# A cross network's input loads rearranged: the second half's remainder transposed on VectorE, fewer transfers on SyncE

## The chip, the cores and the metric

The kernel runs on one core of a Trainium2 chip. The metric is the device time of one execution in microseconds (us). TensorE does the matrix products, ScalarE moves sums out of PSUM and adds a bias, VectorE does the elementwise products and sums, GpSimd makes a few small copies, SyncE issues most of the transfers (DMAs). ScalarE has a queue of its own on which it issues transfers, in order with its other instructions.

## The reference

```python
B, D, L = 4096, 416, 6              # x0: B x D, ws: L x D x D, bs: L x D, all bfloat16
x = x0
for l in range(L):
    x = x0 * (x @ ws[l] + bs[l]) + x
```

## The kernel before, in words

Layers 0 to 4 work on x transposed: features lie on the partitions and rows of the batch along the free axis. The 416 features are three blocks of 128 (the *main* part, XM, index m for an output block and k for an input block) and a *remainder* of 32 (XR). The 4096 rows are two halves s = 0, 1 of four groups g of 512 rows. As 32 features fill only a quarter of the partitions, XR stacks the four groups: partition 32g + r holds feature r of group g. XRd is a copy of XR with its upper and lower 64 partitions exchanged, which the first layer uses for m = 1. The last layer turns round and makes rows of the output directly, from X0rows (x0 as it lies in memory), XLrows (the transposed x of the last layer) and bLr (the last bias row, on partitions 0, 32, 64 and 96).

The loads. SyncE issues, in this order: transposing loads of x0's main part into XM[0] (L75, eight of 512 rows), with the second half's remainder as rows (xrem, L84) after the fifth; weights of layer 1 (L71), the weights' remainder rows (L90), weights of layers 2 to 5, one load for each; x0's rows in four loads (L123); the last bias row in four (L125). ScalarE's queue issues the weights of layer 0, the biases, the first half's remainder in four loads (xrig, L80) and the remainder row of layer 0's weights (WR, L87), which L108 and L110 then copy to three more groups of partitions.

The remainder gets its transposed form in `x0_rem`: four TensorE transposes of a 128x128 tile into PSUM (L155), then one VectorE copy to XR[0] and two to XRd (L158). For the first half the tiles come straight from the four loads; for the second half, GpSimd first copies xrem into their order (L132).

The first layer, `first_layer(s)`, runs for each half. Its PSUM tiles come from a pool of four buffers of 1024 columns (`psum`). pa[0] to pa[2] are the sums of output blocks 0 to 2 for groups 0 and 1, pb[0] to pb[2] those for groups 2 and 3, pr the remainder's. `full` multiplies main blocks (L212), `row` adds the remainder's share (L219). ScalarE empties a tile (`ew_main`, L163), VectorE multiplies by x0 (L164) and adds x (L167); `ew_rem` does the same for pr (L171 to L173). The first half's `x0_rem` stands between the first and second group's products, the second half's behind the first half's pr (`mm_rem`, L191 and L196). Layers 1 to 4 follow in tiles of the same kind (L179, L185), and the last layer (L325 to L353).

The program's scheduler may move instructions of an engine against each other as long as their data allow. `tc.keep_in_program_order(ins)` ties an instruction behind the one that was written before it on its engine; it adds no wait between engines. Each transfer signals its end on one of eight completion semaphores, which are given out in turn in the order of the schedule.

Of the kernel before, what the change touches and what calls it, by code (L numbers as in the profile page):

```python
# [11 lines left out]
BF16 = mybir.dt.bfloat16  # L12
# [4 lines left out]
def kernel(  # L17
# [7 lines left out]
    nc = tc.nc  # L25
    B, D = x0.shape
    L = ws.shape[0]
    P = 128
    NK = 3
    R = D - NK * P  # L30
    assert R == 32 and B == 4096 and D == 416 and L >= 2
    NS = 2
    NG = 4
    CW = 512
    SW = NG * CW
    NBT = B // P
    LL = L - 1

    const = ctx.enter_context(tc.tile_pool(name="const", bufs=1))
    big = ctx.enter_context(tc.tile_pool(name="big", bufs=1))  # L40
# [4 lines left out]
    x0_v = x0.rearrange("(bt p) d -> p bt d", p=P)  # L45
    out_v = out.rearrange("(bt p) d -> p bt d", p=P)

    ident = const.tile([P, P], BF16)
    dz = const.tile([P, 2], FP32)
    ones = const.tile([P, P], BF16)  # L50
    WM = const.tile([P, L, NK, D], BF16)
# [3 lines left out]
    bLr = const.tile([P, D], BF16)  # L55
    bM = const.tile([P, NK, L], FP32)
    bR = const.tile([P, L], FP32)
    X0rows = big.tile([P, NBT, D], BF16)
    XLrows = big.tile([P, NBT, D], BF16)
    scrR = [big.tile([P, 4, P], BF16, name=f"scrR{s}") for s in range(NS)]  # L60
    xrem = big.tile([P, 16, R], BF16)
    xrig = big.tile([P, NS, 4, P], BF16)
    XRd = big.tile([P, NS * CW], BF16)
    XM = [big.tile([P, NK, B], BF16, name=f"XM{i}") for i in range(3)]
    XR = [big.tile([P, NS * CW], BF16, name=f"XR{i}") for i in range(3)]

    def col0(s, g):
        return SW * s + CW * g

    def load_wm(eng, l):  # L70
        eng.dma_start(WM[:, l], ws[l, 0:NK * P, :].rearrange("(k p) n -> p k n", p=P))  # L71

    def load_x0t(s, g):
        c0 = col0(s, g)
        nc.sync.dma_start_transpose(out=XM[0][:, :, c0:c0 + CW], in_=x0[c0:c0 + CW, 0:NK * P])  # L75

    def load_xrem0():
        with nc.allow_non_contiguous_dma(reason="64B row segments"):
            for i in range(4):
                nc.scalar.dma_start(xrig[:, 0, i, :].rearrange("p (g r) -> p g r", g=NG), x0_v[:, i:16:4, NK * P:D])  # L80

    def load_xrem1():
        with nc.allow_non_contiguous_dma(reason="64B row segments"):
            nc.sync.dma_start(xrem[:], x0_v[:, 16:32, NK * P:D])  # L84

    def load_wr0():
        nc.scalar.dma_start(WR[0:R, 0, :], ws[0, NK * P:D, :])  # L87
# [1 line left out]
    def load_wr(eng, g, l0, l1):  # L89
        eng.dma_start(WR[32 * g:32 * g + 32, l0:l1, :], ws[l0:l1, NK * P:D, :].rearrange("l r n -> r l n"))  # L90
# [9 lines left out]
    nc.scalar.dma_start(bsb[:], bs[:, :])  # L100
    load_x0t(0, 1)
    load_xrem0()
    load_wr0()
    nc.scalar.activation(dz[:, 1:2], dz[:, 0:1], ACT.Identity, bias=dz[:, 0:1], scale=1.0)  # L104
    for g in range(1, NG):
        dst, src = WR[32 * g:32 * g + 32, 0, :], WR[0:R, 0, :]
# [4 lines left out]
    for g in range(2, NG):  # L111
        load_x0t(0, g)
    load_x0t(1, 0)
    load_xrem1()
    for g in range(1, NG):
        load_x0t(1, g)
    load_wm(nc.sync, 1)
    for g in range(NG):
        load_wr(nc.sync, g, 1, L)
    for l in range(2, L):  # L120
        load_wm(nc.sync, l)
    for q in range(4):
        nc.sync.dma_start(X0rows[:, 8 * q:8 * q + 8, :], x0_v[:, 8 * q:8 * q + 8, :])  # L123
    for g in range(NG):
        nc.sync.dma_start(bLr[32 * g:32 * g + 1, :], bs[LL:LL + 1, :])  # L125

    def fill_wd(l0, l1):
        for g in range(NG):
            nc.gpsimd.tensor_copy(WD[32 * g:32 * g + 32, l0:l1, g, :], WR[32 * g:32 * g + 32, l0:l1, NK * P:D])

    fill_wd(0, 1)
    nc.gpsimd.tensor_copy(xrig[:, 1].rearrange("p i (g r) -> p i g r", g=NG), xrem[:].rearrange("p (g i) r -> p i g r", g=NG))  # L132
    fill_wd(1, L)

    wps = psum.tile([P, CW], FP32, tag="ps", name="wps")
# [14 lines left out]
        nc.vector.tensor_copy(bM[:], pb[:, 0:NK, 0:L])  # L150
        nc.vector.tensor_copy(bR[:], pb[:, 3, 0:L])

    def x0_rem(s, tpr):
        for i in range(4):
            nc.tensor.transpose(tpr[:, 128 * i:128 * i + 128], xrig[:, s, i, :], ident[:])  # L155
        for dst, src in ((slice(0, P), slice(0, P)), (slice(64, P), slice(0, 64)), (slice(0, 64), slice(64, P))):
            to = XR[0] if dst == src else XRd
            nc.vector.tensor_copy(to[dst, CW * s:CW * s + CW], tpr[src])  # L158

    def ew_main(l, s, m, h, pt, cur, nxt, pin=False):  # L160
        c0 = col0(s, 2 * h)
        t = tpool.tile([P, 2 * CW], BF16, name="t")
        nc.scalar.activation(t[:], pt[:].rearrange("p a b -> p (a b)"), ACT.Identity, bias=bM[:, m, l:l + 1], scale=1.0)  # L163
        prod = nc.vector.tensor_tensor(out=t[:], in0=t[:], in1=XM[0][:, m, c0:c0 + 2 * CW], op=ALU.mult)  # L164
        if pin:
            tc.keep_in_program_order(prod)
        nc.vector.tensor_tensor(out=nxt[:, m, c0:c0 + 2 * CW], in0=t[:], in1=cur[:, m, c0:c0 + 2 * CW], op=ALU.add)  # L167

    def ew_rem(l, s, pr, curR, nxtR):
        tr = tpool.tile([P, 2 * CW], BF16, name="t")  # L170
        nc.scalar.activation(tr[:, 0:CW], pr, ACT.Identity, bias=bR[:, l:l + 1], scale=1.0)  # L171
        nc.vector.tensor_tensor(out=tr[:, 0:CW], in0=tr[:, 0:CW], in1=XR[0][:, CW * s:CW * s + CW], op=ALU.mult)  # L172
        nc.vector.tensor_tensor(out=nxtR[:, CW * s:CW * s + CW], in0=tr[:, 0:CW], in1=curR[:, CW * s:CW * s + CW], op=ALU.add)  # L173
# [15 lines left out]
    def mm_rem(l, s, pr, cur, curR):  # L189
        for g in range(NG):  # L190
            nc.tensor.matmul(pr[32 * g:32 * g + 32, :], lhsT=WD[:, l, g, :], rhs=curR[:, CW * s:CW * s + CW],  # L191
                             start=True, stop=False, tile_position=(0, 32 * g))
        for k in range(NK):
            for g in range(NG):
                c0 = col0(s, g)
                nc.tensor.matmul(pr[32 * g:32 * g + 32, :], lhsT=WM[:, l, k, NK * P:D], rhs=cur[:, k, c0:c0 + CW],  # L196
                      start=False, stop=(k == NK - 1), tile_position=(0, 32 * g))
# [8 lines left out]
    def first_layer(s):  # L206
        cur, curR, nxt, nxtR = XM[0], XR[0], XM[1], XR[1]

        def full(pt, m, h, gl, after_row):
            c0 = col0(s, 2 * h + gl)  # L210
            for k in range(NK):
                nc.tensor.matmul(pt[:, gl, :], lhsT=WM[:, 0, k, 128 * m:128 * m + 128], rhs=cur[:, k, c0:c0 + CW],  # L212
                                 start=(k == 0 and not after_row), stop=(k == NK - 1 and after_row))

        def row(pt, m, h, opens):
            for gl in range(2):
                rg = 32 * ((2 * h + gl) ^ (2 if m == 1 else 0))
                src = XRd if m == 1 else curR
                nc.tensor.matmul(pt[:, gl, :], lhsT=WR[rg:rg + 32, 0, 128 * m:128 * m + 128],  # L219
                                 rhs=src[rg:rg + 32, CW * s:CW * s + CW],  # L220
                                 start=opens, stop=not opens, tile_position=(rg, 0))

        def ph(m):
            return psum.tile([P, 2, CW], FP32, tag="ps", name=f"ph{m}")

        pa = [ph(m) for m in range(NK)]
        if s == 0:
            for m in range(NK):
                full(pa[m], m, 0, 0, False)
            tp0 = psum.tile([P, CW], BF16, tag="ps", name="tpr")  # L230
            x0_rem(0, tp0[:])
            for m in range(NK):
                full(pa[m], m, 0, 1, False)
        else:
            for m in range(NK):
                for gl in range(2):
                    full(pa[m], m, 0, gl, False)
        pb = [ph(0)]
        row(pa[0], 0, 0, False)
        row(pb[0], 0, 1, True)  # L240
        row(pa[2], 2, 0, False)
        row(pa[1], 1, 0, False)
        for m in range(NK):
            ew_main(0, s, m, 0, pa[m], cur, nxt)
        for m in range(NK):
            if m:
                pb.append(ph(m))
            for gl in range(2):
                full(pb[m], m, 1, gl, m == 0)
        row(pb[1], 1, 1, False)  # L250
        row(pb[2], 2, 1, False)
        pr = psum.tile([P, 2, CW], FP32, tag="ps", name="pr")
        mm_rem(0, s, pr[:, 0, :], cur, curR)
        if s == 0:
            x0_rem(1, pr[:, 1, :].bitcast(BF16)[:, 0:CW])
        for m in range(NK):
            ew_main(0, s, m, 1, pb[m], cur, nxt, pin=(s == 0))
        ew_rem(0, s, pr[:, 0, :], curR, nxtR)
# [3 lines left out]
    for s in range(NS):  # L262
        first_layer(s)
# [49 lines left out]
    l = LL  # L313
# [97 lines left out]
```

## Time and profile before

| what | value |
|---|---|
| median of 3 runs | 130.69 us (130.51 to 130.90) |
| profiled execution | 130.58 us |
| its span, first to last instruction | 128.8 us |
| granted TensorE clock | 1.000 over the span |
| first layer, both halves | about 5.8 to 26.8 us |
| layers 1 to 4 | 26.8 to 103.7 us |
| last layer and stores | 103.7 to 128.8 us |
| DMA engines' busy share, 3 to 38 us | 0.9 or more in each slice |
| xrem's load | issued at 10.31 us, landed 4.6 us later |

A row of a timeline gives the start, the duration, the engine, the line, the operation, the tile written and the tile read; a "q" behind an engine's name marks its sequencer, which issues transfers and handles semaphores, and [..] is the engine's idle time before the row and what ended it. "x4" is the number of instructions that the row merges. In the chain of waits each row is a piece of the work that ended last.

### The profile page before, as it was taken

The numbers are of one execution on the slowest core, as the hardware profiler recorded it, in microseconds if no ns is written. First come the engines' busy times: TensorE is split into PE (matmuls) and PEld (weight loads), VectorE is DVE, ScalarE is ACT, GpSimd is POOL, SyncE is SP. The second block draws the span as 40 slices with busy tenths as digits, with TensorE's granted clock in tenths as the row PEclk, the third lists the DMA queues.
The fourth block names the chain that finished last, engine by engine and source line by source line (L and its number), as shares of the span: only waits on it lengthen the run. The fifth ranks groups of instructions, "written<-read, shape, count | busy, mean of one in ns | idle before, by whom it ended". The sixth has DMA issues, their size and how long they took to land.

```text
span 128.8 us, 3973 instructions
## 1 busy us (share of the span) xinstructions
PE 123.6 (96%) x1691; PEld 55.1 (43%) x1691; DVE 106.7 (83%) x195; ACT 86.9 (67%) x99; POOL 6.2 (5%) x18
## 2 busy tenths in 40 slices
PE   7999999999999999999999999999999999999960
PEld 3343443344545444434444544444444445445420
DVE  0023989999999898989898989898989899898991
ACT  0138873887848667848668848668858896569670
POOL 4004300600000000000000000000000000000000
PEclk9999999999999999999999999999999999999999
DMA  4999999999990000000000000000297999985754
GB/s 95 244 231 207 163 153 264 253 328 333 336 291 9 5 0 8 0 0 5 0 5 0 5 0 5 0 5 0 45 163 169 119 237 191 217 261 186 235 178 138
DMA packets 42102, 16.37 MB, mean 127 GB/s; under 512 B 30906, under 2 KB 42084, under 8 KB 42084
## 3 DMA queue, kind: packets, MB, share of 16 engines
q1 hardware_dynamic: 39368, 15.53, 53.9%
q10 hardware_dynamic: 2716, 0.59, 2.5%
q8 instruction: 13, 0.21, 0.7%
q14 instruction: 5, 0.04, 0.1%
HBM read 6.15 MB, written 3.41 MB: 74 GB/s over the span
## 4 chain that ended last, share of the span: by engine, by line
PE 89%; DVE 6%; issue 2%; ACT 1%; DVEq 0%
PE pt L179 49%; PE ph L212 13%; PE py L325 8%; PE pt L185 5%; PE pr L196 5%; PE wps L139 4%; DVE t L353 4%; DVE o L342 2%; PE pr L191 2%; PE ph L219 1%; PE py L331 1%; PE py L334 1%; ACT t L352 1%; PE tpr L155 0%; PE pr L155 0%
## 5 line engine op out<-in xcount | busy, mean ns | idle before, releaser
L179 PE MATMUL pt<-XM,WM 128*32 128x512 bf16 x1152 | 65.2, 379 | 0.0
L163 ACT ACTIVATE t<-pt,bM 128x1024 bf16<-128x1024 f32 x48 | 49.6, 1115 | 18.5 <-PE pt L185 18.5
L164 DVE TENSOR_TENSOR t<-t,XM 128x1024 bf16<-128x1024 bf16 x60 | 41.4, 690 | 5.2 <-ACT t L163 5.2
L167 DVE TENSOR_TENSOR XM<-t,XM 128x1024 bf16<-128x1024 bf16 x60 | 41.8, 697 | 3.4
L179 PEld LDWEIGHTS <-WM 128*32 128x32 bf16 x1152 | 29.7, 97 | 33.8 <-issue 5.1
L352 ACT CAST t<-py 128x416 bf16<-128x416 f32 (+1 forms) x23 | 14.8, 642 | 4.8 <-PE py L325 2.6
L325 PE MATMUL py<-WM,XM 128*128 128x416 bf16 x96 | 17.7, 340 | 0.0
L212 PE MATMUL ph<-XM,WM 128*128 128x512 bf16 x72 | 16.5, 381 | 0.0
L163 ACT ACTIVATE t<-ph,bM 128x1024 bf16<-128x1024 f32 x12 | 12.5, 1114 | 3.4 <-PE ph L219 3.4
L325 PEld LDWEIGHTS <-XM 128*128 128x128 bf16 x96 | 9.0, 98 | 8.5 <-issue 1.4
L353 DVE TENSOR_TENSOR t<-t,X0rows 128x416 bf16<-128x416 bf16 (+1 forms) x23 | 10.4, 457 | 1.2 <-ACT t L352 1.2
L342 DVE TENSOR_TENSOR o<-t,XLrows 128x416 bf16<-128x416 bf16 (+1 forms) x23 | 10.4, 456 | 0.0
L212 PEld LDWEIGHTS <-WM 128*128 128x128 bf16 x72 | 6.7, 98 | 8.4 <-issue 1.1
L171 ACT ACTIVATE t<-pr,bR 128x512 bf16<-128x512 f32 x10 | 6.4, 685 | 2.7 <-PE pr L196 2.1
L196 PE MATMUL pr<-XM,WM 128*32 128x512 bf16 x120 | 8.2, 379 | 0.0
L185 PE MATMUL pt<-XR,WR 32*128 32x512 bf16 x96 | 7.3, 379 | 0.0
L139 PE MATMUL wps<-const-bfloat16-1.0 128*128 128x512 bf16 (+1 forms) x12 | 4.9, 592 | 0.8 <-PEq L395 0.8
L104 ACT ACT_TABLE_LOAD x1 | 1.3, 1283 | 6.0 <-DMA XM<-in_x_dram 6.0
L173 DVE TENSOR_TENSOR XR<-t,XR 128x512 bf16<-128x512 bf16 x10 | 4.2, 425 | 0.7
L196 PEld LDWEIGHTS <-WM 128*32 128x32 bf16 x120 | 3.2, 97 | 3.0
L150 DVE CAST bM<-pb 128x18 f32<-128x18 bf16 x1 | 0.2, 177 | 5.1 <-PE pb L149 5.1
L172 DVE TENSOR_TENSOR t<-t,XR 128x512 bf16<-128x512 bf16 x10 | 4.2, 420 | 0.0
(38 smaller groups left out, 33.5 us busy)
## 6 DMA issues: line engine op xcount, KB each, us to landing
X0rows<-in_x_dram SPq DMA_DIRECT2D x4, 832.0 KB, 11.5
out_dram<-o SPq DMA_DIRECT2D x9, 208.0 KB, 2.5
WM<-in_ws_dram SPq DMA_DIRECT2D x5, 312.0 KB
out_dram<-o SPq DMA_DIRECT2D x13, 104.0 KB, 1.9
WR<-in_ws_dram SPq DMA_DIRECT2D x4, 130.0 KB, 4.1
WM<-in_ws_dram ACTq DMA_DIRECT2D x1, 312.0 KB
XM<-in_x_dram SPq DMA_TRANSPOSE x8, 4.9
xrig<-in_x_dram ACTq DMA_DIRECT2D x4, 32.0 KB, 4.2
```

The lines of the kernel that those rows point to most:

```text
L139: nc.tensor.matmul(wps[:, 0:cols], lhsT=warm[:, 0:P], rhs=warm[:, 0:cols], start=True, stop=True)
L163: nc.scalar.activation(t[:], pt[:].rearrange("p a b -> p (a b)"), ACT.Identity, bias=bM[:, m, l:l + 1], scale=1.0)
L164: prod = nc.vector.tensor_tensor(out=t[:], in0=t[:], in1=XM[0][:, m, c0:c0 + 2 * CW], op=ALU.mult)
L167: nc.vector.tensor_tensor(out=nxt[:, m, c0:c0 + 2 * CW], in0=t[:], in1=cur[:, m, c0:c0 + 2 * CW], op=ALU.add)
L179: nc.tensor.matmul(pts[g // 2][32 * q:32 * q + 32, g % 2, :], lhsT=WM[:, l, k, 128 * m + 32 * q:128 * m + 32 * q + 32], rhs=cur[:, k, c0:c ...
L185: nc.tensor.matmul(pts[g // 2][:, g % 2, :], lhsT=WR[32 * g:32 * g + 32, l, 128 * m:128 * m + 128], rhs=curR[32 * g:32 * g + 32, CW * s:CW ...
L196: nc.tensor.matmul(pr[32 * g:32 * g + 32, :], lhsT=WM[:, l, k, NK * P:D], rhs=cur[:, k, c0:c0 + CW], start=False, stop=(k == NK - 1), tile ...
L212: nc.tensor.matmul(pt[:, gl, :], lhsT=WM[:, 0, k, 128 * m:128 * m + 128], rhs=cur[:, k, c0:c0 + CW], start=(k == 0 and not after_row), sto ...
L325: nc.tensor.matmul(py[:, 0:D], lhsT=cur[:, k, q_cols(q, g)], rhs=WM[:, l, k, :], start=((not closes) and k == 0), stop=(closes and k == NK ...
L342: tc.keep_in_program_order(nc.vector.tensor_tensor(out=o, in0=t, in1=xl, op=ALU.add))
L352: nc.scalar.copy(tv, src)
L353: tc.keep_in_program_order(nc.vector.tensor_tensor(out=tv, in0=tv, in1=X0rows[:, b, :], op=ALU.mult))
```

## The change

Four edits are made together.

1. The second half's remainder is loaded with partition p holding rows 16p to 16p + 15 of the half, and VectorE transposes it block by block (32x32) straight into XR[0]; XRd's halves are then copied from XR[0]. TensorE's four transposes and GpSimd's copy for that half are gone.
2. xrem's load moves from SyncE to ScalarE's queue. It is written behind the first half's `x0_rem`, and a memset of one element of each partition of xrem, placed on VectorE behind that step's copies, makes it wait for them.
3. The last bias row comes in one load to four partitions instead of four loads. It moves to ScalarE's queue, tied behind xrem's load.
4. The weights of layers 2 to 5 come in three loads (one for each input block k, all four layers) instead of four, and x0's rows in one load instead of four.

All new steps of `x0_rem0` and `x0_rem1` on VectorE are kept in program order.

```diff
-    xrig = big.tile([P, NS, 4, P], BF16)
+    xrig = big.tile([P, 4, P], BF16)
...
+    def pin(ins):
+        tc.keep_in_program_order(ins)
...
     def load_xrem1():
+        pin(nc.vector.memset(xrem[:, 0, 0:1], 0.0))
         with nc.allow_non_contiguous_dma(reason="64B row segments"):
-            nc.sync.dma_start(xrem[:], x0_v[:, 16:32, NK * P:D])
+            pin(nc.scalar.dma_start(xrem[:], x0[SW:2 * SW, NK * P:D].rearrange("(p t) r -> p t r", p=P)))
...
     load_x0t(1, 0)
-    load_xrem1()
     for g in range(1, NG):
         load_x0t(1, g)
     load_wm(nc.sync, 1)
     for g in range(NG):
         load_wr(nc.sync, g, 1, L)
-    for l in range(2, L):
-        load_wm(nc.sync, l)
-    for q in range(4):
-        nc.sync.dma_start(X0rows[:, 8 * q:8 * q + 8, :], x0_v[:, 8 * q:8 * q + 8, :])
-    for g in range(NG):
-        nc.sync.dma_start(bLr[32 * g:32 * g + 1, :], bs[LL:LL + 1, :])
+    for k in range(NK):
+        nc.sync.dma_start(WM[:, 2:L, k, :], ws[2:L, P * k:P * k + P, :].rearrange("l p n -> p l n"))
+    nc.sync.dma_start(X0rows[:], x0_v)
...
-    nc.gpsimd.tensor_copy(xrig[:, 1].rearrange("p i (g r) -> p i g r", g=NG), xrem[:].rearrange("p (g i) r -> p i g r", g=NG))
...
-    def x0_rem(s, tpr):
+    def x0_rem0(tpr):
         for i in range(4):
-            nc.tensor.transpose(tpr[:, 128 * i:128 * i + 128], xrig[:, s, i, :], ident[:])
+            nc.tensor.transpose(tpr[:, 128 * i:128 * i + 128], xrig[:, i, :], ident[:])
         for dst, src in ((slice(0, P), slice(0, P)), (slice(64, P), slice(0, 64)), (slice(0, 64), slice(64, P))):
             to = XR[0] if dst == src else XRd
-            nc.vector.tensor_copy(to[dst, CW * s:CW * s + CW], tpr[src])
+            pin(nc.vector.tensor_copy(to[dst, 0:CW], tpr[src]))
+        load_xrem1()
+        pin(nc.scalar.dma_start(bLr[0:P:32, :], bs[LL:LL + 1, :].to_broadcast([NG, D])))
+
+    def x0_rem1():
+        pin(nc.vector.transpose(XR[0][:, CW:2 * CW].rearrange("p (j t) -> p t j", t=16), xrem[:]))
+        for dst, src in ((slice(64, P), slice(0, 64)), (slice(0, 64), slice(64, P))):
+            pin(nc.vector.tensor_copy(XRd[dst, CW:2 * CW], XR[0][src, CW:2 * CW]))
...
-            x0_rem(1, pr[:, 1, :].bitcast(BF16)[:, 0:CW])
+            x0_rem1()
```

More of the change, by code (lines that the diff above doesn't have):

```diff
@@ L79, in load_xrem0 @@
             for i in range(4):
-                nc.scalar.dma_start(xrig[:, 0, i, :].rearrange("p (g r) -> p g r", g=NG), x0_v[:, i:16:4, NK * P:D])
+                nc.scalar.dma_start(xrig[:, i, :].rearrange("p (g r) -> p g r", g=NG), x0_v[:, i:16:4, NK * P:D])
     def load_xrem1():
+        pin(nc.vector.memset(xrem[:, 0, 0:1], 0.0))
         with nc.allow_non_contiguous_dma(reason="64B row segments"):
-            nc.sync.dma_start(xrem[:], x0_v[:, 16:32, NK * P:D])
+            pin(nc.scalar.dma_start(xrem[:], x0[SW:2 * SW, NK * P:D].rearrange("(p t) r -> p t r", p=P)))
     def load_wr0():
@@ L230, in first_layer @@
             tp0 = psum.tile([P, CW], BF16, tag="ps", name="tpr")
-            x0_rem(0, tp0[:])
+            x0_rem0(tp0[:])
             for m in range(NK):
```

## The prediction

> **What bounds the kernel now.** I read the totals first, then the chain of waits through the first 30 us, then the timeline of each engine between 5 and 22 us, where all edits but the merged loads act.
>
> ```profile
> PE 123.6 (96%) x1691; PEld 55.1 (43%) x1691; DVE 106.7 (83%) x195; ACT 86.9 (67%) x99; POOL 6.2 (5%) x18
> PE 89%; DVE 6%; issue 2%; ACT 1%; DVEq 0%
> ```
>
> TensorE is busy for 96% of the span. The chain in order of time says more: without a gap it stays on TensorE from 0.77 to 115.65 us, and only the last 13 us belong to VectorE and the stores. So whatever TensorE no longer does before 115 us is won, and every stall of TensorE is lost, one for one.
>
> ```profile
> 15.73 0.33 PE pr L191 x4
> 16.06 0.65 PE pr L196 x12
> 16.71 0.33 PE pr L155 x4
> 17.04 3.88 PE ph L212 x18
> ```
>
> This is the chain at the end of the first half's first layer. The four matmuls of L155 are the transposes of the second half's remainder, and they take 0.33 us of it.
>
> The timeline of ScalarE's queue and engine (start, duration):
>
> ```profile
> 1.18 0.69 ACTq L100 DMA_DIRECT2D bsb<-in_bs_dram  x1
> ...
> 2.32 0.66 ACTq L80 DMA_DIRECT2D xrig<-in_x_dram  x1
> 3.01 0.56 ACTq L80 DMA_DIRECT2D xrig<-in_x_dram  x1
> 4.01 0.37 ACTq L80 DMA_DIRECT2D xrig<-in_x_dram  x1
> 5.64 0.34 ACTq L87 DMA_DIRECT2D WR<-in_ws_dram  x1
> ...
> 9.66 1.10 ACT L108 COPY WR<-WR 32x416 bf16<-32x416 bf16 x2 [2.07 <-DMA WR<-in_ws_dram]
> 11.09 4.13 ACT L163 ACTIVATE t<-ph,bM 128x1024 bf16<-128x1024 f32 x4 [0.33 <-PE ph L219]
> ```
>
> The L163 at 11.09 empties pa[0]. TensorE needs that buffer again soon: all four PSUM buffers are held by pa[0] to pa[2] and pb[0], and the next tile, pb[1], takes pa[0]'s. Its matmuls are in this row:
>
> ```profile
> 11.35 4.06 PE L212 MATMUL ph<-XM,WM 128*128 128x512 bf16 x18
> ```
>
> Eighteen matmuls in some 3.9 us start 0.216 us apart. The first six are pb[0]'s, so pb[1] starts at 11.35 + 6 x 0.217 = 12.65. The activation ends at 11.09 + 1.11 = 12.20. With some 0.05 us for the signal, ScalarE may come 0.40 us late before TensorE stands still.
>
> **The change part by part.**
>
> *Transposes taken from TensorE:* 4 instructions, 0.33 us by the chain, all on the path: -0.33. What is next behind them is ready: pa[0] of the second half takes pb[0]'s buffer, emptied by 15.2, and the first transposed load of that half has landed at 8.91 + 4.6 = 13.5.
>
> *Transposes given to VectorE:* L158's three copies (17.08 to 18.39, after 0.48 us of waiting for TensorE) give way to one transpose of 128x512 and two copies of 64x512. No row shows a VectorE transpose. A 128x512 copy takes 0.42 and GpSimd's rearranging copy of that shape 1.06, so I take 0.7; the copies stay at 0.43 each. That is 1.56 against 1.31 us, but it starts without the 0.48 us wait. VectorE's product behind it starts near 18.3 as before. TensorE reads the result at 20.86 (L219), 2.5 us later, so this costs nothing; at the upper ends (1.06, then 1.31 more behind the adds) it still ends before 19.5. The Trainium skill (VectorE: DVE Perf Modes, The three transpose paths) gives 311 ns for 128x128; four times that, an estimate of 1.24 us, leaves the sum as it is.
>
> *GpSimd's copy removed:* 1.06 us at 15.00, off the path. The add that ran beside it took 0.98 instead of 0.69; that returns to VectorE, which waits for nothing there. Zero.
>
> *Merged loads on SyncE:* the transfer work is the same bytes in the same row lengths. Layer 1's weights stay as they are; the merged weights are first read when the third layer starts at 46 us and x0's rows after 103, while the DMA slices are empty from 39 us. Zero, with 7 us of cover for the weights. SyncE also loses xrem's 0.58 us issue, so the next three transposed loads come up to 0.6 us earlier. The tightest, read from 17.7 us on, had 0.7 us to spare; zero.
>
> *xrem's load moved to ScalarE's queue:* now it waits for a memset on VectorE behind the two XRd copies. They end at 9.99; with the 0.06 us of the memset at L93, the issue starts at 10.1. Queued behind it on ScalarE are the last bias row's load and then the L163 of 11.09. ScalarE's sequencer runs ahead of the engine: its wait for the first L163 is recorded at 9.7 (the row below), while the second L108 copy only starts at 10.2. So the copies don't delay the issue, and the issue blocks the sequencer, not the copies.
>
> ```profile
> L163 ACTq EVENT_SEMAPHORE  x52: 17/17/17, 9.7 to 102.5; - x52
> ```
>
> The same issue took 0.58 on SyncE: done at 10.7. This alone is free, since L163's input is ready only at 11.04. xrem landed 4.6 us after its issue; now that is near 14.7, and VectorE wants it at 16.3. Zero.
>
> *The bias row's load behind it:* this is where I see a cost. SyncE's timeline:
>
> ```profile
> 10.31 0.58 SPq L84 DMA_DIRECT2D xrem<-in_x_dram  x1
> 10.95 3.08 SPq L75 DMA_TRANSPOSE XM<-in_x_dram  x1
> ...
> 28.64 2.48 SPq L123 DMA_DIRECT2D X0rows<-in_x_dram  x1
> 31.16 2.48 SPq L125 DMA_DIRECT2D bLr<-in_bs_dram  x1
> ```
>
> A transfer of 832 bytes (bLr) occupies its queue 2.48 us when it is issued right behind a transfer of 1,024 segments, and 0.25 when it isn't (the median of the four issues at L125). The transposed load right behind xrem is the longest of its eight (3.08, median 1.95). On ScalarE's queue the issues right behind 512 segments took 0.66 and 0.56, the others 0.34 to 0.39. In these rows a large transfer is accepted quickly and its successor pays. xrem has 2,048 segments of 64 bytes, and bLr is now its successor. Bounds: 0.25 (nothing is paid) to 3.08. Scaling the extra 0.2 to 0.3 us per 512 segments by four gives 1.0 to 1.5; scaling the whole 0.66 gives 2.6. The nearest row by operation is bLr's own 2.48, but there the queue was full, and ScalarE's is empty. I take 1.8: bLr's issue ends at 12.5. Then L163 starts at 12.55 instead of 11.09, pa[0] is free at 12.55 + 1.11 + 0.05 = 13.71, and pb[1] stalls 13.71 - 12.65 = 1.06 us. The following tiles add nothing: L163 repeats every 1.0 us, a tile's matmuls take 1.3.
>
> A rule of the Trainium skill bears on the same place (Perfetto Trace Analysis, DMA Instruction — HWDGE): descriptor generation is locked for one sequencer's exclusive use, and the issue is over when all descriptors are generated. The trace speaks against the lock here: two xrig issues (2.32 to 2.98, 3.01 to 3.57) lie inside one SyncE issue of 2.61 us. By the rule xrem would wait for SyncE's transposed load; that is the third rival.
>
> *Sum:* -0.33 + 1.06 = +0.73 us. The profiled execution took 130.58 (span 128.80, 1.78 around it), so 131.3; it lies 0.11 below the median of 130.69, which gives 131.4 on that scale.
>
> **The rivals.**
>
> *No blocking (not slower).* If the empty ScalarE queue accepts bLr in its 0.25 to 0.39 us, the issue ends by 11.1, inside the 0.40 us of slack, and only -0.33 is left: 130.36. The deciding point is bLr's end at 11.45. For it: xrig's four issues put 2,048 segments in flight from this queue, none over 0.66. Against it: xrem brings them in one transfer.
>
> *The semaphore's turn.* Transfers share eight completion semaphores in turn, and an issue waits until the transfer that had the semaphore before has landed: WR's at 5.64 starts when the first transposed load lands (0.74 + 4.9). Fewer transfers shift the turns. If bLr's falls on the small first-half loads, landed by 9.7, or on the fourth transposed load (10.9), nothing is added; if on the second half's first (13.5), bLr ends near 13.9, L163 starts at 13.95 and the stall is 13.95 + 1.16 - 12.65 = 2.46: 132.8. For it: that load stands only a few places from the turns that I count.
>
> *The lock.* xrem's issue begins after the transposed load that SyncE issues from 10.3, up to 3.08 us: 13.4, plus 0.58 and 0.25, so 14.2. The stall is 2.76: 133.1. The row above is against it.
>
> *xrem lands late.* From 19.2 us on (20.5 less 1.3 for transpose and first copies), its landing stops TensorE's L219; at 20.5 that is 1.3 us on top of the sum: 132.7. The landing of 4.6 us is against it.
>
> **How the numbers follow.** Blocking by xrem 0.50; no blocking 0.24; the semaphore 0.18; the lock 0.04; late xrem 0.04. The likeliest gives 131.4, its own range 130.6 to 132.2 (bLr's end between 11.75 and 13.3). For 8 in 10 I reach down to the no-blocking case, 130.2, and up through the semaphore's, 132.9. A measurement of this kernel tells about 0.3%, 0.39 us, from no change. No blocking is -0.25%: I count 0.14 of it as the same and 0.10 as faster. Of the blocking case 0.10 stays under +0.39 (bLr's end before 12.15). So faster 0.10, same 0.24, slower 0.40 + 0.18 + 0.04 + 0.04 = 0.66.
>
> **What would show it.** In the changed profile: no L155 between L196 and L212 near 16 us; one xrem issue on ScalarE's queue at 10.1, a bLr issue behind it of over 1 us, the first L163 after 12, and TensorE idle before pb[1] near 12.65, released by ScalarE's L163. A bLr issue under 0.5 us with L163 still at 11.1 would make the forecast wrong, and the gain 0.33. A bLr start, not a long issue, near 13.5 would be the semaphore. Waits of the third layer for WM, or of VectorE for xrem at 16.3, would show the covers wrong.

## The result and the profile after

The changed kernel takes 132.32 us (median of 6 executions, 132.15 to 132.74) against 130.74 for the kernel before, run beside it (6 executions, 130.47 to 130.90). The ratio is 1.0128, with an interval of 1.0108 to 1.0149: slower, by 1.58 us. The profiled execution took 132.24 us with a span of 130.4, against 130.58 and 128.8.

In the code of the changed kernel the lines named ahead lie six further down: `ew_main` is L169, `full` L218, `row` L225, `mm_rem` L197 and L202. The loads of xrem and bLr are L88 and L159, the VectorE transpose L162.

The totals and the chain's shares, from the page of the changed kernel:

```profile
PE 122.6 (94%) x1685; PEld 55.0 (42%) x1687; DVE 107.9 (83%) x196; ACT 86.6 (66%) x99; POOL 4.9 (4%) x17
PE 82%; DVE 6%; DMA 4%; issue 2%; ACTq 2%; ACT 2%; DVEq 0%
```

Before, the chain named TensorE alone from 0.77 to 115 us. Now DMA and ScalarE's sequencer (ACTq) have shares in it, but these lie ahead of 8.25 us, where TensorE's first transposes wait for xrig's loads, and shift the start by only 0.07 us (table below). The new piece that counts is one activation on ScalarE (ACT), in the chain in order of time (start, duration, what):

```profile
11.86 1.04 PE ph L218 x4
12.90 0.03 issue
12.93 1.12 ACT t L169
14.05 0.04 issue
14.10 2.75 PE ph L218 x12
16.84 0.33 PE ph L225 x4
17.17 0.33 PE pr L197 x4
17.50 0.65 PE pr L202 x12
18.15 2.05 PE ph L218 x9
```

Two things are to be seen. The transposes that stood behind L196 are gone: L202 is followed by L218 at once. And at 12.9 the chain leaves TensorE for an activation and comes back at 14.10. The timeline of ScalarE says what held that activation:

```profile
9.73 0.54 ACT L112 COPY WR<-WR 32x416 bf16<-32x416 bf16 x1 [2.01 <-DMA WR<-in_ws_dram]
10.12 0.66 ACTq L88 DMA_DIRECT2D xrem<-in_x_dram  x1
10.29 0.54 ACT L112 COPY WR<-WR 32x416 bf16<-32x416 bf16 x1
11.57 1.31 ACTq L159 DMA_DIRECT2D bLr<-in_bs_dram  x1
12.93 4.13 ACT L169 ACTIVATE t<-ph,bM 128x1024 bf16<-128x1024 f32 x4 [2.10 <-PE ph L218]
```

xrem's issue is where it was expected, and it took 0.66 us. bLr's issue began only at 11.57, 0.79 us behind it, and then lasted 1.31. It ended at 12.88, and L169 started at 12.93 instead of 11.09. TensorE's timeline and its list of waits show what that costs:

```profile
11.42 1.47 PE L218 MATMUL ph<-XM,WM 128*128 128x512 bf16 x5
14.10 2.75 PE L218 MATMUL ph<-XM,WM 128*128 128x512 bf16 x12 [1.21 <-ACT t L169]
```
```profile
PE ph L218 <- ACT t L169: 1.2, 1, 1.2
```

Six matmuls of pb[0], 0.217 us apart, would have let pb[1] begin at 12.72; it began at 14.10, so it is 1.38 us late. (The row lists five of the six, as some matmul records can be missing. The idle time shown is shorter than the delay, since the end of the last matmul before it is modelled.) The steps of the prediction behind bLr's issue hold to 0.01 us: 12.88 + 0.05 = 12.93 for the activation, and 12.93 + 1.11 + 0.05 = 14.09 for pb[1].

On VectorE, the transpose and the two XRd copies:

```profile
18.07 2.35 DVE L162 STREAM_TRANSPOSE XR<-xrem 128x512 bf16<-128x512 bf16 x1
20.45 0.61 DVE L164 COPY XRd<-XR 64x512 bf16<-64x512 bf16 x2
```

The transpose takes 2.35 us. First-layer matmuls don't wait for it, but VectorE carries the delay on, and in layer 1 the second half's remainder is late once (its last VectorE operation, L179, runs from 34.16 to 34.58 us; TensorE begins with it at 34.63):

```profile
33.82 0.22 PE pr L197 x4
34.03 0.65 PE pr L202 x12
34.68 0.35 PE pr L197 x4
35.03 0.65 PE pr L202 x12
```

The second group of L197 holds the chain for 0.35 us, the first for 0.22. In the kernel before both take 0.21 to 0.22:

```profile
32.60 0.21 PE pr L191 x4
33.47 0.22 PE pr L191 x4
```

The merged loads, on SyncE's timeline, are issued sooner than before (all by 25.3 us, before by 34.5), x0's rows have landed at 40.2 us in both kernels, and nothing waits for them:

```profile
19.73 5.00 SPq L124 DMA_DIRECT2D WM<-in_ws_dram  x3
24.77 0.51 SPq L125 DMA_DIRECT2D X0rows<-in_x_dram  x1
```

Put together along the chain, before to after (starts of the same matmul group, the last VectorE operation, the end of the span):

| stretch | before | after | difference |
|---|---|---|---|
| first matmul of `row` | 10.66 | 10.73 | +0.07 |
| from there to the first half's last `row` | 4.68 | 6.05 | +1.37 |
| from the first half's `mm_rem` (its second line, L196 and L202) to layer 1 | 10.70 | 10.48 | -0.22 |
| layer 1 to the end of the last VectorE operation | 99.60 | 99.72 | +0.12 |
| last VectorE operation to the end of the span | 2.61 | 2.88 | +0.27 |

The sum is +1.61 us, the whole difference of the two spans. (The stretch between the last `row` and that line of `mm_rem` is 0.55 in both.)

### The profile page after: what moved, and what is told of

Read it like the earlier page. It is cut to its first block, busy times and chain, and to the rows that moved or that the text cites. A ratio compares the mean times of both kernels' runs of the same rounds, so it can differ in the third digit from the quotient of the medians.

```text
span 130.4 us, 3952 instructions
## 1 busy us (share of the span) xinstructions
PE 122.6 (94%) x1685; PEld 55.0 (42%) x1687; DVE 107.9 (83%) x196; ACT 86.6 (66%) x99; POOL 4.9 (4%) x17
## 4 chain that ended last, share of the span: by engine, by line
PE 82%; DVE 6%; DMA 4%; issue 2%; ACTq 2%; ACT 2%; DVEq 0%
PE pt L185 49%; PE ph L218 11%; PE py L331 8%; PE pt L191 5%; PE pr L202 5%; DMA xrig<-in_x_dram 4%; DVE t L359 4%; PE pr L197 2%; DVE o L348 2%; PE ph L225 1%; PE py L337 1%; ACT t L169 1%; ACTq L83 1%; PE py L340 1%; ACT t L358 1%
## 5 line engine op out<-in xcount | busy, mean ns | idle before, releaser
L169 ACT ACTIVATE t<-pt,bM 128x1024 bf16<-128x1024 f32 x48 | 49.5, 1114 | 18.3 <-PE pt L191 18.3
L218 PE MATMUL ph<-XM,WM 128*128 128x512 bf16 x70 | 16.4, 379 | 2.1 <-ACT t L169 1.2
L169 ACT ACTIVATE t<-ph,bM 128x1024 bf16<-128x1024 f32 x12 | 12.5, 1112 | 5.3 <-PE ph L225 3.2
L218 PEld LDWEIGHTS <-WM 128*128 128x128 bf16 x72 | 6.8, 98 | 10.8 <-issue 3.5
L202 PE MATMUL pr<-XM,WM 128*32 128x512 bf16 x120 | 8.2, 379 | 0.0
L179 DVE TENSOR_TENSOR XR<-t,XR 128x512 bf16<-128x512 bf16 x10 | 4.3, 435 | 0.7
L138 PE MATMUL wps<-const-bfloat16-1.0 128*128 128x512 bf16 (+1 forms) x12 | 3.9, 495 | 0.8 <-PEq L401 0.8
L202 PEld LDWEIGHTS <-WM 128*32 128x32 bf16 x120 | 3.2, 97 | 2.9
L197 PE MATMUL pr<-XR,WD 128*32 128x512 bf16 x40 | 3.9, 382 | 0.0
```

## The experiments

Theory A was that bLr's issue on ScalarE's queue holds the first activation; theory B that the VectorE transpose, or xrem's own issue on that queue, is the main cost. Four kernels came first, each the changed kernel but for the edit shown. Times of before beside them: 130.55 us.

**e1_blr_sync**: bLr at the end of SyncE's queue.

```diff
     nc.sync.dma_start(X0rows[:], x0_v)
+    nc.sync.dma_start(bLr[0:P:32, :], bs[LL:LL + 1, :].to_broadcast([NG, D]))
...
-        pin(nc.scalar.dma_start(bLr[0:P:32, :], bs[LL:LL + 1, :].to_broadcast([NG, D])))
```

> The changed kernel (132.3 us), with the last bias row's load alone moved back to the end of SyncE's queue. Theory A (ScalarE's first L169 is held by that load's issue, which waits for a semaphore and then for xrem's descriptors): L169 starts at 11.1 us again, TensorE does not stand before pb[1], and the 1.4 us of that stall come back: 130.9 us, within 0.3% of before (130.7). Theory B (xrem's issue on ScalarE's queue, or the 2.35 us transpose on VectorE, is what costs): the time stays near 132.3.

Measured 131.10 us, ratio 1.0044 (1.0029 to 1.0058). The first activation starts at 11.03 and TensorE has no gap from 11.28 on; layer 1 begins at 26.30 (before 26.59). So 1.2 us come back, and A holds. But TensorE is 0.3 us ahead of the kernel before and the whole is 0.55 us behind it: something else is lost, after TensorE.

**e2_blr_early**: the same line on ScalarE's queue right behind WR's load, at 6.16 us.

```diff
+    pin(nc.scalar.dma_start(bLr[0:P:32, :], bs[LL:LL + 1, :].to_broadcast([NG, D])))
...
-        pin(nc.scalar.dma_start(bLr[0:P:32, :], bs[LL:LL + 1, :].to_broadcast([NG, D])))
```

> The changed kernel, with the last bias row's load on ScalarE's queue still, but issued early, behind the weights' remainder row (about 6.1 us), before xrem's. Theory A: its issue takes 0.3 to 0.7 us there, where ScalarE waits for data anyway, L169 starts at 11.1 and the time is 130.9. Theory B: near 132.3, as the queue and xrem's place are the same. If any transfer on ScalarE's queue costs its issue time on TensorE's path, 131.2 to 131.6.

Measured 131.17 us, ratio 1.0045 (1.0029 to 1.0061). The issue lasts 0.61 us there, and the activation starts at 11.17. Not the queue, but the place behind xrem makes the issue long.

That the time is that of e1 is chance. One transfer more ahead of it shifts the turn of SyncE's fourth transposed load: it now has the semaphore of the second, which lands at 8.66, so that its issue starts at 8.68 instead of 6.88 in the changed kernel. It lands at 12.41, and TensorE waits for it:

```profile
8.68 1.42 SPq L75 DMA_TRANSPOSE XM<-in_x_dram  x1
12.45 3.40 PE L218 MATMUL ph<-XM,WM 128*128 128x512 bf16 x15 [0.16 <-DMA XM<-in_x_dram]
```

The second stretch of the table above is 0.37 us longer in e2 than in e1, while e2's end, from the last VectorE operation on, is 0.54 us shorter than e1's (2.78 and 3.32). What makes the end long in e1 comes below.

**e3_turn_more** and **e4_turn_less** leave bLr where the change put it and change how many transfers come ahead of it, and so which earlier transfer had its completion semaphore.

```diff
 e3: -    load_wm(nc.sync, 1)
     +    nc.sync.dma_start(WM[:, 1, 0:1, :], ws[1, 0:P, :].rearrange("(k p) n -> p k n", p=P))
     +    nc.sync.dma_start(WM[:, 1, 1:NK, :], ws[1, P:NK * P, :].rearrange("(k p) n -> p k n", p=P))
 e4: -    load_wm(nc.sync, 1)
     +    for k in range(NK):
     +        nc.sync.dma_start(WM[:, 1:L, k, :], ws[1:L, P * k:P * k + P, :].rearrange("l p n -> p l n"))
          ...
     -    for k in range(NK):
     -        nc.sync.dma_start(WM[:, 2:L, k, :], ws[2:L, P * k:P * k + P, :].rearrange("l p n -> p l n"))
```

> The changed kernel, with layer 1's weights in two loads instead of one, so that one more transfer takes its turn before the last bias row's: that now has the semaphore of the second half's first transposed load (lands near 13.5 us) instead of the first half's fourth (11.5). Theory A with the semaphore as a real term: the bias row's issue starts at 13.5 instead of 11.57. If the issue's length of 1.3 us is time in which xrem's descriptors are made, it is 0.3 to 0.4 now, L169 starts near 13.95, a microsecond later than in the changed kernel: 133.3. If the length is its own, L169 starts near 14.9: 134.3. Theory B, or the semaphore without a part in it: 132.3.

> The changed kernel, with layer 1's weights taken into the three merged loads, so that one transfer less takes its turn before the last bias row's: that has the semaphore of the weights' remainder row (landed at 9.7 us) and need not wait. If the issue lasts until xrem's descriptors are made, it starts at 10.8 and still ends between 12.4 and 12.9: 131.8 to 132.3 us. If its length of 1.3 us is its own, it ends at 12.1 and L169 starts 0.8 us earlier than in the changed kernel: 131.5. Without blocking of either kind (an issue of 0.35 us): L169 at 11.2 and 130.9. Theory B: 132.3.

Measured 133.95 us for e3 (five executions from 133.53 to 134.29, one at 135.64), ratio 1.0285 (1.0244 to 1.0326; 1.026 by the medians), and 131.90 for e4, ratio 1.0101 (1.0082 to 1.0121). For e3 that is above the 133.3 of the first case expected, though its issue is short and its activation starts at 13.97 as that case has it; the end of the program, 3.27 us against 2.88 in the changed kernel, has a part in this. ScalarE's timeline of e3, with SyncE's row beside it from a window of the whole timeline, and TensorE's stall:

```profile
13.34 0.59 ACTq L160 DMA_DIRECT2D bLr<-in_bs_dram  x1
12.59 2.70 SPq L75 DMA_TRANSPOSE XM<-in_x_dram  x1
15.14 2.75 PE L219 MATMUL ph<-XM,WM 128*128 128x512 bf16 x12 [2.34 <-ACT t L170]
```

and those of e4:

```profile
10.16 0.66 ACTq L88 DMA_DIRECT2D xrem<-in_x_dram  x1
10.85 1.81 ACTq L158 DMA_DIRECT2D bLr<-in_bs_dram  x1
13.88 2.75 PE L217 MATMUL ph<-XM,WM 128*128 128x512 bf16 x12 [0.96 <-ACT t L168]
```

In e4 no semaphore holds bLr: its issue begins right behind xrem's, and it lasts 1.81 us. In e3 the semaphore is that of a transposed load of the second half; the issue waits for it until 13.34 and then lasts 0.59, with a SyncE issue running beside it all the while. So the long issue goes with what xrem left behind, over some 2.5 us after xrem's issue begins. A rival is that bLr waits for SyncE, whose transposed load beside it ends its issue at 12.63 in both kernels, 0.25 us ahead of bLr's end in the changed kernel and 0.03 us ahead in e4. Against it stand e3's bLr (13.34 to 13.93, inside a SyncE issue from 12.59 to 15.29) and the WR issue of the changed kernel (5.77 to 6.11, inside one from 4.94 to 6.83): both ended while SyncE's went on. In the changed kernel both waits overlap: the semaphore until 11.57, the rest of xrem until 12.88. The semaphore's own share is 12.88 - 12.66 = 0.22 us.

What was open now was the end of the program. In e1 the last VectorE operation ends at 125.90 (before: 126.19), yet the span ends at 129.22 (before: 128.80). Theory M laid that on the smaller number of transfers, theory D on the VectorE transpose. Times of before beside these four: 130.54 us.

**e5_merged_only** (the kernel before with the merged loads alone) and **e6_dve_only** (the kernel before with the VectorE transpose alone: `x0_rem1` of the change in place of `x0_rem(1, ...)`, GpSimd's copy left out, no load merged or moved):

```diff
 e5: -    for l in range(2, L):
     -        load_wm(nc.sync, l)
     -    for q in range(4):
     -        nc.sync.dma_start(X0rows[:, 8 * q:8 * q + 8, :], x0_v[:, 8 * q:8 * q + 8, :])
     -    for g in range(NG):
     -        nc.sync.dma_start(bLr[32 * g:32 * g + 1, :], bs[LL:LL + 1, :])
     +    for k in range(NK):
     +        nc.sync.dma_start(WM[:, 2:L, k, :], ws[2:L, P * k:P * k + P, :].rearrange("l p n -> p l n"))
     +    nc.sync.dma_start(X0rows[:], x0_v)
     +    nc.sync.dma_start(bLr[0:P:32, :], bs[LL:LL + 1, :].to_broadcast([NG, D]))
 e6: -            nc.sync.dma_start(xrem[:], x0_v[:, 16:32, NK * P:D])
     +            nc.sync.dma_start(xrem[:], x0[SW:2 * SW, NK * P:D].rearrange("(p t) r -> p t r", p=P))
```

> The kernel before with the merged loads alone (weights 3 to 6 in three loads, x0's rows in one, the last bias row in one, all on SyncE's queue; transposes by TensorE as before). Theory M (fewer, larger transfers change the order of the completion semaphores and so the tail after the last VectorE operation): the last VectorE operation ends where it did (126.2 us) and the time rises by about 0.5, to 131.1. Theory D (the tail belongs to the VectorE transpose or to something that it shifts): the time is that of before, 130.5 to 130.7.

> The kernel before with the second half's remainder transposed by VectorE alone; every load stays on its queue and in its order (the remainder's own on SyncE, with the new pattern). Theory M: TensorE comes 0.3 us earlier to the last layer (no four transposes), the tail is that of before, and the time is 130.2 to 130.4. Theory D: TensorE 0.3 us earlier, but the tail 0.7 to 0.8 longer, 131.0.

Measured 131.28 us for e5, ratio 1.0050 (1.0038 to 1.0062), and 130.41 for e6, ratio 0.9988 (0.9979 to 0.9997). M holds as to the place: loads that nobody waits for, all landed by 41 us, cost 0.74 us at 126 us when they are merged. The reason that its expectation gives, the order of the semaphores, is tested with e9 below. The VectorE transpose by itself is a small gain.

**e7_count_same**: e1 with x0's rows in eight loads, so that there are 64 transfers again.

```diff
-    nc.sync.dma_start(X0rows[:], x0_v)
+    for q in range(8):
+        nc.sync.dma_start(X0rows[:, 4 * q:4 * q + 4, :], x0_v[:, 4 * q:4 * q + 4, :])
```

> The changed kernel with the last bias row alone back at the end of SyncE's queue (as e1_blr_sync), and x0's rows in eight loads in place of one, so that the program again has 64 transfers and the last store the same completion semaphore as in the kernel before. Theory M: the tail is that of before, 130.2 to 130.4. Theory D, or a tail that does not hang on the order of the semaphores: as e1_blr_sync, 131.0 to 131.2.

Measured 130.58 us, ratio 1.0002 (0.9993 to 1.0011): 0.52 us come back with seven more transfers. The time lies 0.18 us above the range that M gave.

**e8_pe_transposes**: the changed kernel with the second half's TensorE transposes, VectorE copies, GpSimd copy and xrem pattern of before.

```diff
...
-        pin(nc.vector.transpose(XR[0][:, CW:2 * CW].rearrange("p (j t) -> p t j", t=16), xrem[:]))
-        for dst, src in ((slice(64, P), slice(0, 64)), (slice(0, 64), slice(64, P))):
-            pin(nc.vector.tensor_copy(XRd[dst, CW:2 * CW], XR[0][src, CW:2 * CW]))
+        nc.gpsimd.tensor_copy(xrig[:, 1].rearrange("p i (g r) -> p i g r", g=NG), xrem[:].rearrange("p (g i) r -> p i g r", g=NG))
+        for i in range(4):
+            nc.tensor.transpose(tpr[:, 128 * i:128 * i + 128], xrig[:, 1, i, :], ident[:])
+        for dst, src in ((slice(0, P), slice(0, P)), (slice(64, P), slice(0, 64)), (slice(0, 64), slice(64, P))):
+            to = XR[0] if dst == src else XRd
+            pin(nc.vector.tensor_copy(to[dst, CW:2 * CW], tpr[src]))
```

> The changed kernel with the second half's remainder transposed by TensorE as before (GpSimd's copy, four transposes, VectorE copies); all loads as in the changed kernel. If ScalarE's late bias load alone makes the loss (theory A): TensorE's stall stays at 1.2 us, the four transposes cost 0.33 again, and the time is 132.3 to 132.7. If the VectorE transpose of 2.35 us makes a good part of it (theory B): 131.5 or less.

Measured 132.10 us, ratio 1.0114 (1.0099 to 1.0128), 0.2 us under the range expected. TensorE's stall is 1.08 us by its idle time (1.21 in the changed kernel), the transposes take their 0.22 again (10.70 against 10.48 us in the third row of the table), and the 0.12 of layer 1 is gone. Theory B falls: the VectorE transpose accounts for nothing of the loss beyond that 0.12, and in e1 and e6, where the same transpose starts at 16.2 and 16.4 us instead of 18.07, layer 1 and what follows take the 99.60 us of before.

How can a load at 25 us cost half a microsecond at 126? I followed SyncE's instructions in the trace of each kernel. In every one, also in the kernel before, SyncE pauses for 0.44 to 0.47 us between its 79th and its 80th recorded instruction, counted from the start. Which instruction that is depends on how many came before. Theory P: where it is the last store on SyncE, that store is issued 0.3 us late, together with ScalarE's last one, and the program ends with it. P was then set against theory T, by which the turn of the semaphores alone does it. Times of before beside these four: 130.53 us.

**e9_turn_kept**: as e7, but nine loads. The semaphores' turn is then exactly that of e1, while SyncE has eight more instructions.

```diff
-    nc.sync.dma_start(X0rows[:], x0_v)
+    for q in range(9):
+        a, b = (4 * q, 4 * q + 4) if q < 7 else (14 + 2 * q, 16 + 2 * q)
+        nc.sync.dma_start(X0rows[:, a:b, :], x0_v[:, a:b, :])
```

> As e1_blr_sync (last bias row at the end of SyncE's queue), with x0's rows in nine loads in place of one: 65 transfers, so the turn of the eight completion semaphores is exactly that of e1_blr_sync (57) and the last store has the same one, but SyncE has eight more instructions. Theory P (a pause of 0.45 us that comes before SyncE's 80th recorded instruction in every trace so far; in e1 and e5 it meets the last store on SyncE, here it would meet the store four earlier, which has time to catch up): the last VectorE operation ends at 125.9, the tail behind it is 2.7 to 2.8 us in place of 3.3, the time 130.5 to 130.7. Theory T (the semaphores' turn alone sets the tail): as e1, 131.0 to 131.2.

Measured 130.56 us, ratio 1.0000 (0.9989 to 1.0010): P. The end of the timeline of e1 (start, duration; the two stores are the last of SyncE and of ScalarE):

```profile
125.24 0.66 DVE L348 TENSOR_TENSOR o<-t,XLrows 128x416 bf16<-128x416 bf16 x2
125.93 0.40 ACTq L349 DMA_DIRECT2D out_dram<-o  x1
125.95 0.33 SPq L349 DMA_DIRECT2D out_dram<-o  x1
```

and of e9, where the SyncE row merges the last two SyncE stores, at 125.09 and 125.67:

```profile
125.09 0.90 SPq L351 DMA_DIRECT2D out_dram<-o  x2
125.26 0.66 DVE L350 TENSOR_TENSOR o<-t,XLrows 128x416 bf16<-128x416 bf16 x2
125.95 0.38 ACTq L351 DMA_DIRECT2D out_dram<-o  x1
```

In both the second-to-last VectorE sum ends near 125.6 us. In e9 SyncE stores it at once, in e1 only when the last sum is done too. The two stores then start together in e1 and land 2.1 and 2.3 us after their issue, instead of 1.7 each in e9; so 0.3 us of delay become 0.6 at the end. Over all kernels, from one trace of each:

```text
kernel              transfers  SyncE's 80th instruction is   last VectorE  end of  from one to
                               (or stands before)            op ends       span    the other
before                  64     fifth-last store              126.19        128.80    2.61
after                   57     behind the last store         127.53        130.41    2.88
e1_blr_sync             57     last store                    125.90        129.22    3.32
e2_blr_early            57     behind the last store         126.40        129.18    2.78
e3_turn_more            58     last store                    128.48        131.75    3.27
e4_turn_less            56     behind the last store         127.22        130.33    3.11
e5_merged_only          57     last store                    126.06        129.52    3.46
e6_dve_only             64     fifth-last store              126.11        128.80    2.69
e7_count_same           64     fourth-last store             125.93        128.71    2.78
e8_pe_transposes        57     behind the last store         127.58        130.36    2.78
e9_turn_kept            65     fifth-last store              125.92        128.63    2.71
e10_xrem_sync           57     last store                    126.04        129.35    3.31
e11_dense_bias          64     fifth-last store              125.82        128.75    2.93
e12_dve_more            72     ninth-last store              125.83        128.42    2.59
```

The four kernels whose last SyncE store meets the pause need 3.27 to 3.46 us for the end, the others 2.59 to 3.11. (In e4, the 3.11, one store's issue took 0.95 us instead of 0.33.) The merged load of x0's rows alone does not lengthen the end: the changed kernel, e2 and e8 have it too, and need 2.78 to 2.88.

**e10_xrem_sync**: xrem back on SyncE behind the fifth transposed load, bLr where the change has it.

```diff
-        pin(nc.vector.memset(xrem[:, 0, 0:1], 0.0))
...
-            pin(nc.scalar.dma_start(xrem[:], x0[SW:2 * SW, NK * P:D].rearrange("(p t) r -> p t r", p=P)))
+            (nc.sync.dma_start(xrem[:], x0[SW:2 * SW, NK * P:D].rearrange("(p t) r -> p t r", p=P)))
...
+    load_xrem1()
...
-        load_xrem1()
+        pin(nc.vector.memset(bLr[:, 0:1], 0.0))
```

> The changed kernel with the second half's remainder loaded on SyncE's queue, in its old place, and the last bias row still on ScalarE's queue behind the XRd copies' place (a VectorE write to its tile comes before it). Its predecessor on ScalarE's queue is then the 32-row weight load of 6 us. Theory A1 (the bias load's issue is long because the remainder's 2048 segments are still being worked off on the same queue): the issue lasts 0.4 to 0.65 us, TensorE has no stall at the second bank, and the time is that of e1, 131.0 to 131.2 (SyncE again has the instruction count of e1). Theory A2 (a one-row load with four targets is slow in itself there): 1.2 to 1.8 us, a stall of 0.5 to 1 us, 131.6 to 132.

Measured 131.11 us, ratio 1.0036 (1.0022 to 1.0049), with this row:

```profile
10.14 0.61 ACTq L159 DMA_DIRECT2D bLr<-in_bs_dram  x1
```

A1: without xrem ahead of it the four-target row is issued in 0.61 us, L169 starts at 11.19 and TensorE has no stall. As xrem's issue on SyncE (10.38) came behind it, this run does not tell whether xrem would also hold it from the other queue.

**e11_dense_bias** and **e12_dve_more** are versions meant to beat the kernel before: its loads and queues, with the VectorE transpose. e11 loads xrem in four parts so that the transpose writes densely, and bLr in one load; e12 is e6 with x0's rows in twelve loads.

```diff
 e11: -            nc.sync.dma_start(xrem[:], x0_v[:, 16:32, NK * P:D])
      +            for g in range(NG):
      +                nc.sync.dma_start(xrem[32 * g:32 * g + 32], x0[SW + CW * g:SW + CW * g + CW, NK * P:D].rearrange("(t j) r -> j t r", j=32))
          ...
      +        tc.keep_in_program_order(nc.vector.transpose(XR[0][:, CW:2 * CW], xrem[:].rearrange("p t r -> p (t r)")))
 e12: -    for q in range(4):
      -        nc.sync.dma_start(X0rows[:, 8 * q:8 * q + 8, :], x0_v[:, 8 * q:8 * q + 8, :])
      +    for q in range(12):
      +        a, b = (4 * q, 4 * q + 4) if q < 4 else (8 + 2 * q, 10 + 2 * q)
      +        nc.sync.dma_start(X0rows[:, a:b, :], x0_v[:, a:b, :])
```

> The kernel before with the VectorE transpose, the remainder's rows loaded in four loads so that the transpose reads and writes densely, and the last bias row in one load on SyncE (64 transfers, as before). If the 2.35 us of the VectorE transpose come from its strided output: 1.0 to 1.3 us here; if it is the price of 128x512 in itself: 2.35 again. Time 130.3 to 130.5 either way, since no one waits for it on this path; a last bias load or more loads of the remainder that come late would show as a stall.

> e6_dve_only with x0's rows in twelve loads in place of four (72 transfers, same turn at the end, eight more instructions on SyncE). Theory P: the pause before SyncE's 80th instruction meets a store eight places from the end, the last stores are issued right when VectorE is done, and the tail is at most that of before: 130.1 to 130.4. Theory T: as e6, 130.4. A cost of the more transfers themselves would show as above 130.6.

Measured 130.34 us for e11, ratio 0.9983 (0.9973 to 0.9993), and 130.31 for e12, ratio 0.9982 (0.9972 to 0.9991). Both beat the kernel before by 0.2 us. Their intervals overlap with that of e6, which has the VectorE transpose alone, so a gain of what they add to it is not shown. e11's VectorE timeline:

```profile
16.13 0.70 DVE L160 STREAM_TRANSPOSE XR<-xrem 128x512 bf16<-128x512 bf16 x1
```

A transpose of the same shape takes 0.70 us when its output is dense and 2.35 us when neighbouring output elements lie 32 bytes apart. Neither of the two lengths expected for it, 1.0 to 1.3 us or 2.35 again, came out; that the output pattern sets the price did.

## Why the prediction came out too small

The direction and the place were right: slower, by an activation held behind bLr's issue on ScalarE's queue, with TensorE stalled at pb[1]. The size was not: +0.73 us was forecast, and the two spans differ by 1.61. The step that failed is the sum: its one cost, bLr's stall, was set too low, the gain on TensorE too high, and two terms put at nothing, the end of the program behind the merged loads and the longer VectorE transpose, were not nothing. That the time still lies inside the range for 8 in 10 is no merit of these terms, since the range reached so far up for the semaphore's case, which fell on another load. Term by term:

- *Transposes off TensorE, -0.33.* Measured -0.22, in the changed kernel and in e1, e6 and e9 alike. The four pieces in the chain lasted 0.33, but the following tile started 0.24 us after L155, not 0.33 (16.64 and 16.88 in TensorE's timeline of before). The term was read from the chain, whose pieces don't overlap as pipelined matmuls do. Mis-sized by 0.11.
- *bLr's issue, ending at 12.5, stall 1.06.* Measured 12.88 and 1.38, +1.37 along the chain. Mis-sized by 0.31, the largest term. The 1.8 us that I took for the issue is what e4 measures (1.81); as no row gave it, and the two scalings gave 1.0 to 1.5 and 2.6, this was luck. What was missing is the wait ahead of it. I named the semaphore's turn as a rival and wrote that on the fourth transposed load, landed at 10.9, it would add nothing. It fell on that load, and that load lands later than I read: its last signal comes at 11.51 us in the trace of before and at 11.55 in the changed kernel's. The two waits are not added to each other, since both run beside xrem's work; together they end 0.22 us later than the issue alone in e4. The remaining 0.16 of the 0.38 us is the later start of the issue without that wait, 10.85 in e4 instead of 10.7.
- *The VectorE transpose, 0.7 us, "costs nothing".* It took 2.35, beyond my upper end of 1.06, and cost 0.12 in layer 1, there only together with the late activation (e1 and e6 lose nothing). By chance the 0.7 is the dense transpose of e11; the rows I scaled from, a copy and a GpSimd rearrangement, could not show the price of a strided output. The estimate of 1.24 that I worked out from the Trainium skill's 311 ns (VectorE: DVE Perf Modes, The three transpose paths) lies between the two, and neither form agrees with it.
- *Merged loads, zero.* As loads they did cost nothing. But I asked only who waits for the data, not what fewer instructions do to SyncE later. In the changed kernel the end is 0.27 us longer. Of this 0.15 is the last store's own way, 1.90 us from issue to landing instead of 1.75 in the trace of before, and some 0.11 is that its semaphore now stands third among SyncE's five closing waits, so that two more follow it; that split is read from the two traces and was not tested by itself, and the kernels whose last store misses the pause differ among themselves by as much (2.59 to 2.93, e4 left out). The pause was harmless in the change itself, since SyncE had no more stores; in e1 it cost 0.5 us (against e7 and e9).
- *The start*, +0.07, is how the first loads landed in these two executions.

The errors are 0.11 + 0.31 + 0.12 + 0.27 + 0.07 = 0.88, which is 1.61 - 0.73.

Of the other rivals: *no blocking* needed bLr's end before 11.45 and fell. *The lock* fell as well: xrem's issue began at 10.12, ahead of the end of one SyncE issue at 10.31, and was over at 10.78, long before the end of the next at 12.63; e3's bLr and WR's issue lie wholly inside a SyncE issue. The rule of the Trainium skill (Perfetto Trace Analysis, DMA Instruction — HWDGE) that one sequencer holds descriptor generation for itself does not agree with these rows. Its point that an issue lasts until its descriptors are made does not account for the lengths either: the 2,048 segments of xrem took 0.66, and bLr's four rows 1.81 behind them and 0.61 without them (e10). *xrem landing late*: it landed at 16.29 us, 1.6 later than I thought, and VectorE was not ready for it before 18.07.

The merged loads also show how an effect can be hidden by another. In the changed kernel the pause lies behind the last store. As soon as bLr is put back on SyncE, the obvious repair, the pause moves onto the last store, and of the 1.63 us by which the last VectorE operation then ends sooner (125.90 for 127.53), 0.44 are lost again behind it.

## What to carry to other kernels

A small transfer tied behind a large one on an engine that also computes can hold that engine, here until some 2.5 us after the large one's issue began; issue it before, or from an engine with nothing to do. Neither was free here: the early issue (e2) shifted the turn of a load that TensorE needed, and the issue on SyncE (e1) moved the pause onto the last store. Ask of each transfer in a tight place which earlier transfer had its completion semaphore, and read that transfer's landing, not its issue. And if a kernel ends with stores, compare the stretch from the last operation to the end of the span whenever instructions are added to or removed from the storing queue, however early they run.

## What the hardware showed that was not expected

- SyncE's pause of 0.44 to 0.47 us stands before its 80th recorded instruction in all 14 traces, whatever that instruction is. Within 1 us behind it each trace has at least one packet of 8,192 bytes in a DMA queue that the profile calls "instruction". That fits a change to the next block of instructions, but no run here shows it. The Trainium skill (Runtime: NRT & Kernel Launch, Instruction fetch mechanics) describes such refills as mostly hidden; here the pause is seen.
- An issue behind 2,048 segments of 64 bytes on the same queue takes 1.81 us right behind it, 1.31 when it comes 1.45 us after the large one began, and 0.59 after 3.3 us. Four loads of 512 segments one behind another (e11, on SyncE) took 0.58, 0.47, 0.49 and 0.49.
- A VectorE transpose with a strided output costs 3.4 times the dense one (2.35 and 0.70 us for 128x512 bfloat16).
